# Two shared pools of PSUM slots and a new list of operations in a recurrence with a highway layer

## The chip, the core and the metric

The kernel runs on one core of a Trainium2 chip. The metric is device time in microseconds (us), the median over repeated runs. The engines are TensorE (PE: matmuls and transposes, results go to PSUM), VectorE (DVE), ScalarE (ACT), GpSimd (POOL), and SyncE (SP), which here only issues DMA transfers. Each engine works through its own queue in order and waits on semaphores for the others.

## What is computed

```python
sig = 1.0 / (1.0 + np.exp(-f_logit))          # x, f_logit: (4, 6336, 256)
f = lower_bound + (1.0 - lower_bound) * sig
i = 1.0 - f
for t in range(S):                            # for each of 4 sequences
    h = f[:, t] * h + i[:, t] * x[:, t]
    y[:, t] = h
H = np.maximum(y @ w_h, 0.0)                  # 25344 tokens of 256
T = 1.0 / (1.0 + np.exp(-(y @ w_t + b_t)))
out = T * H + (1.0 - T) * y
```

Inputs and output are float32. The recurrence runs along time, the highway layer works on each token by itself.

## The kernel before

The work is cut into 25 units: 24 of 1024 tokens (6 stretches of time for each of 4 sequences) and a last one of 768 that holds the rest of all four sequences. The channels (256) are two halves of 128 partitions. The first three units are cut into smaller pieces at the front (`CUTS`), the last into two pieces throughout.

With u = sigmoid(-f_logit), f = 1 - (1 - lower_bound) u and i x = (1 - lower_bound) u x. The factor (1 - lower_bound), `cc`, is taken out of the scan and put into the weights (`w_sb`) and a diagonal matrix (`diag`); `ncc` is its negative. Each step of a unit has a letter, and the string `PLAN` is a list of letters written out by hand: for each letter the next instance of that step is emitted, and `pin` keeps the emitted order on each engine. So `PLAN` gives the order of all five queues.

| letter | engine | step (line) |
|---|---|---|
| L, X, R | SP | load f_logit, load x (L106), store out (L297); Q: the weights (L120) |
| U | ACT | u = sigmoid(-f_logit), 128x2048 (L149) |
| P | POOL | bv = u x, four per unit (`product`, L155) |
| A, F | PE, ACT | transpose u into uT (L186), then f = 1 + ncc uT (L193); per half |
| B, S | PE, DVE | transpose bv into bT (L202), then the scan y = f y + bT (L217); per half |
| W | DVE | fold cc into the weights (L143), twice |
| Z, T | PE, ACT | zp = w_t y (L232), t = sigmoid(zp + b_t) (L238); per half |
| G, D | PE, DVE | gp = w_h y (L232), d = max(ncc y, gp) (L243); per half |
| E, H | DVE, POOL | e = d t, its columns divided between DVE (L258) and POOL (L155); both halves at once |
| O | PE | op = diag y + e, transposed back to tokens (L276, L277); two groups `q` of four blocks per unit |
| C, V | ACT, DVE | copy op to o (L291); V takes half of each copy in the last three pieces |

Before, each of the five kinds of product has one PSUM tile (`bufs=1`, tag = kind): uT and bT one bank each, zp, gp and op two banks each, eight in all. A product waits until the reader of the last one of its kind is done. `SHARE` is the number of columns of each half of e that POOL takes (448 of 1024; DVE takes the other 576, so a row of the profile has 2 x 576 = 1152). `gpsimd_mul` makes a POOL multiplication wait for DVE's e before it in the list. The pools in SBUF hold five f_logit tiles, five x tiles and eight o tiles. The DMA transfers share eight semaphores, so that each waits for the one eight before it.

Of the kernel before, what the change touches and what calls it, by code (L numbers as in the profile page):

```python
# [19 lines left out]
def kernel(  # L20
# [43 lines left out]

    HELPED = 3

    first = ctx.enter_context(tc.tile_pool(name="first", bufs=1))
# [14 lines left out]
    def pin(ins):  # L84
        return tc.keep_in_program_order(ins)

    def pairs(t):

        return t.rearrange("p (k j) d -> p k (j d)", j=2)

    def inner(t):

        return t.rearrange("p k d j -> p k j d")
# [1 line left out]
    def tokens(src, u, j0, j1, j):  # L95

        np_, _, b, per, a = units[u]
        if per == NB:
            return src[b, a + j0 * np_:a + j1 * np_, :].rearrange("(k p j) d -> p k (j d)", p=np_, j=j)
        return src[b + j0 // per:b + j1 // per, a:a + per * np_, :].rearrange("b (p j) d -> p b (j d)", j=per)  # L100

    def load(i, name, src):
        u, j0, j1 = fronts[i]
        np_ = units[u][0]
        t = fs[i][name] = new(name, [NB, D], FP32)
        pin(nc.sync.dma_start(pairs(t[:np_, :j1 - j0]), tokens(src, u, j0, j1, 2)))  # L106

    def shape(piece):

# [43 lines left out]
    def gpsimd_mul(out_, a, b):  # L153

        ins = pin(nc.gpsimd.tensor_mul(out_, a, b))  # L155
        while port:
            tc.add_manual_dep(ins.ins, port.pop().ins.name, mybir.DependencyInfo(
                mybir.DependencyClass.Sync, mybir.DependencyReason.DATA), reason="shared port")

    def product(i, k):  # L160
        np_, _ = shape(fronts[i])
        if k == 0:
            fs[i]["bv"] = new("bv", [NB // 2, D, 2], BF16)
        gpsimd_mul(inner(fs[i]["bv"][:np_, k:k + 1])[:, 0], fs[i]["u"][:np_, 2 * k:2 * k + 2],
                   fs[i]["xt"][:np_, 2 * k:2 * k + 2])

    def width(piece):
        np_, nb = shape(piece)
# [3 lines left out]

        return ((0,), (1,)) if width(piece) > 512 else ((0, 1),)

    def psum(piece, m, s, key, dtype):

        t = ps1.tile([P, NB * P], dtype, tag=key, name=key)
        for c, h in enumerate(halves(piece)[m]):
            s[key, h] = t[:, c * 512:c * 512 + width(piece)]
            yield s[key, h], h  # L180

    def decay_pe(i, m):
        np_, nb = shape(fronts[i])
        for uT, h in psum(fronts[i], m, fs[i], "uT", FP16):
            for j in range(nb):
                pin(nc.tensor.transpose(uT[:, j * np_:(j + 1) * np_], fs[i]["u"][:np_, j, h * P:(h + 1) * P],  # L186
                                        ident_h[:np_, :np_]))

    def decay_act(i, h):

        np_, N = shape(fronts[i])[0], width(fronts[i])
        f = fs[i]["f", h] = new("f", [NB * P], FP16)
        pin(nc.scalar.activation(f[:, :N].rearrange("p (k q j) -> p k q j", q=np_, j=2),  # L193
                                 fs[i]["uT", h].rearrange("p (k j q) -> p k q j", q=np_, j=2), AF.Identity,
                                 scale=ncc[:, h:h + 1], bias=1.0))

    def b_pe(i, m):
        np_, nb = shape(fronts[i])
        for bT, h in psum(fronts[i], m, fs[i], "bT", BF16):

            for k in range(nb // 2):
                pin(nc.tensor.transpose(bT[:, 2 * k * np_:2 * (k + 1) * np_].bitcast(FP32),  # L202
                                        fs[i]["bv"][:np_, k, h * P:(h + 1) * P].rearrange("p d j -> p (d j)").bitcast(FP32),
                                        ident_f[:np_, :np_]))

# [17 lines left out]
        u, j0, j1 = backs[j]  # L223
        return ys[u][:, :, j0 * units[u][0]:j1 * units[u][0]]

    def ffn_pe(j, m, key, k):
        N = width(backs[j])
        for p, h in psum(backs[j], m, bs[j], key, FP32):
            for ki in range(NH):
                for a in range(0, N, 512):  # L230
                    e = min(a + 512, N)
                    pin(nc.tensor.matmul(p[:, a:e], w_sb[:, k, ki, h * P:(h + 1) * P], y_of(j)[:, ki, a:e],  # L232
                                         start=ki == 0, stop=ki == NH - 1))
# [9 lines left out]
        pin(nc.vector.scalar_tensor_tensor(bs[j]["d"][:, m, :width(backs[j])], y_of(j)[:, m], ncc[:, m:m + 1],  # L243
                                           bs[j]["gp", m], op0=ALU.mult, op1=ALU.max))

    SHARE = 448

    def shared(j):

# [5 lines left out]
        return (bs[j][key][:, :, a:e] for key in "edt")  # L255

    def e_dve(j):
        port.append(pin(nc.vector.tensor_mul(*e_cols(j, 0, width(backs[j]) - shared(j)))))  # L258

    def e_pool(j):  # L260
        gpsimd_mul(*e_cols(j, width(backs[j]) - shared(j), width(backs[j])))

    QB = NB // 2

    def o_pe(j, q):

        op = bs[j]["op", q] = ps1.tile([P, QB, D], FP32, tag="op", name="op")
        (np_, nb), y = shape(backs[j]), y_of(j)
        j0, j1 = q * QB, min((q + 1) * QB, nb)
        g = min(j1 - j0, units[backs[j][0]][3])  # L270
        for k in range(j0, j1):
            b, i = divmod(k - j0, g)
            cols = slice((j0 + b * g) * np_ + i, (j0 + (b + 1) * g) * np_, g)
            for h in range(NH):
                o = op[:np_, k - j0, h * P:(h + 1) * P]
                pin(nc.tensor.matmul(o, y[:, h, cols], diag[:, h], start=True, stop=False))  # L276
                pin(nc.tensor.matmul(o, bs[j]["e"][:, h, cols], ident_b, start=False, stop=True))  # L277

    def copied(j, q):

        g = min(QB, shape(backs[j])[1] - q * QB)
        return g, g // 2 if j >= len(backs) - HELPED else g

    def o_copy(j, q, engine):
        np_ = shape(backs[j])[0]
        if ("o", q) not in bs[j]:
            bs[j]["o", q] = new("o", [QB, D], FP32)
        g, a = copied(j, q)
        part = slice(0, a) if engine is nc.scalar else slice(a, g)
        copy = nc.scalar.copy if engine is nc.scalar else nc.vector.tensor_copy  # L290
        pin(copy(bs[j]["o", q][:np_, part], bs[j]["op", q][:np_, part]))  # L291

    def store(j, q):
        u, j0, _ = backs[j]
        a, (g, _) = j0 + q * QB, copied(j, q)
        per = min(g, units[u][3])
        pin(nc.sync.dma_start(tokens(out_bsd, u, a, a + g, per),  # L297
                              bs[j]["o", q][:units[u][0], :g].rearrange("p (k j) d -> p k (j d)", j=per)))

    def each(pieces, count):  # L300
        return [(i, k) for i, piece in enumerate(pieces) for k in range(count(piece))]

    def groups(piece):
        return -(-shape(piece)[1] // QB)


    kinds = {
# [1 line left out]
        "X": (lambda i, _: load(i, "xt", x), each(fronts, lambda p: 1)),  # L309
        "Q": (lambda i, k: load_weights(k), [(0, 0), (0, 1)]),  # L310
        "U": (lambda i, _: gate(i), each(fronts, lambda p: 1)),
        "P": (product, each(fronts, lambda p: shape(p)[1] // 2)),
        "A": (decay_pe, each(fronts, lambda p: len(halves(p)))),
        "F": (decay_act, each(fronts, lambda p: NH)),
        "B": (b_pe, each(fronts, lambda p: len(halves(p)))),
        "S": (scan, each(fronts, lambda p: NH)),
        "W": (lambda i, h: weights(h), [(0, 0), (0, 1)]),
        "Z": (lambda j, m: ffn_pe(j, m, "zp", 1), each(backs, lambda p: len(halves(p)))),
        "T": (t_act, each(backs, lambda p: NH)),
        "G": (lambda j, m: ffn_pe(j, m, "gp", 0), each(backs, lambda p: len(halves(p)))),  # L320
        "D": (d_dve, each(backs, lambda p: NH)),
        "E": (lambda j, _: e_dve(j), each(backs, lambda p: 1)),
        "H": (lambda j, _: e_pool(j), [(j, 0) for j in range(len(backs)) if shared(j)]),
        "O": (o_pe, each(backs, groups)),
        "C": (lambda j, q: o_copy(j, q, nc.scalar), each(backs, groups)),
        "V": (lambda j, q: o_copy(j, q, nc.vector), [p for p in each(backs, groups) if p[0] >= len(backs) - HELPED]),
        "R": (store, each(backs, groups)),
    }

    PLAN = (  # L330
        "XLLXLXQQLXUUAPFFBAPSSUFFBASSWLLXLXPFFUPBAPFFUUPWSSLLXXLXPPGABZPPFFTDSSGABZUFFTDSSEAGBZFUFUTHPPPPPPDS"
        "SOGABZCFTDSSAOGHPPPPFABZDSUFCTGBZALLXLXXLLRUTUFDSBGEESDOZBAGCTUFSDPPPPHZOBASTCFGZOBAPPPPHTCFDSZGOABD"
        "ESTUCFGZOABTFCDZAGOHPPPPFTCSDEEAGBOZXXRRLRRRRLLXFUCTDSAGBOZDSPHPPPFCTAOBZGESDFCOBATUFPPPPHPPZGATFCSD"
        "BZGAOTFCUSDPPHBZGAOXRRXXLRXLRRRTFCSDEBGAZOFTCESDABZGOPPPPPPHFTUCSDABGZOSEDPPHFTCABZGOFTUCSDRRXLLXRRR"
        "XBZGAOSDTFCBAGOZPHPPPPSDEFUTCBAGZOSDFTCABZGOPPHPPSDEFTCXLLRRRRBGAOZESDUFCTBOAGZSPHPPPPPPUFTCBADSGZOB"
        "FTCDESAGOZBHPPPPUCFTDSOGAZBCTFDSOGZBAHPCTUFDEESGZOABXRRRXRLLXLLRRDSTFCPPPPPHZGAOBTFCDSZGOBAUTCDSPPPH"
        "ZGODEFTCUBZAGOFTCESDABZGOFTCUSDPPHPPHPPPABZGOSDRXRRLRRRLXTCFBZOAGSEDTCFBZAGOTUCFSDBZGOAPPPPPHTCSDEZB"
        "OGFCTAOESDPHPPUCBZGOSDFTCBAZGORRRXRRRRXPHPUFTCSDEBAGZOSDFFTCABZGOFTCPPHRRRSSDEZGOBTFCRDGOZHSDDESCROT"
        "TCEVRGZOTTCDDVROEVCROCVR"
    )  # L340
    assert all(PLAN.count(k) == len(places) for k, (_, places) in kinds.items())
    todo = {k: iter(places) for k, (_, places) in kinds.items()}
    for k in PLAN:
        kinds[k][0](*next(todo[k]))
# [1 line left out]
_INS = ['x', 'f_logit', 'lower_bound', 'moe_w_h', 'moe_w_t', 'moe_b_t']  # L346
_OUTS = [((25344, 256), 'float32')]
# [25 lines left out]
```

## Time and profile before

| | us |
|---|---|
| median of 8 runs | 220.27 (219.81 to 221.81) |
| the profiled execution, whole | 221.08 |
| its span in the profile | 219.3 |

| what | value |
|---|---|
| scan (L217, 128x1024), mean | 2340 ns x40 |
| d (L243, 128x1024), mean | 1259 ns x48 |
| e on DVE, 1152 columns | 760 ns x24 |
| e on POOL, 896 columns | 1944 ns x24 |
| product bv on POOL | 1176 ns x96 |
| u (L149, 128x2048) | 1954 ns x21 |
| f, t, copy on ACT (128x1024) | 1176, 1166, 1060 ns |
| bytes moved | 78.4 MB, 52.4 read and 26.0 written |

The span is from the first to the last instruction of the profiled execution. A line of the timeline gives the start in us, the duration in us, engine and line of the kernel, operation, output and inputs, shape and count; in brackets stands how long the engine was idle before it, and what ended the wait. Durations of neighbours on one engine overlap a little, so the distance from start to start is what an operation costs there.

### The profile page before, as it was taken

Reading aid. Unit: us, or ns where it says so; the run is one execution under the profiler, and the core shown is the slowest. Engines: PE = TensorE matmul, PEld = TensorE weight load, DVE = VectorE, ACT = ScalarE, POOL = GpSimd, SP = SyncE. Lnnn points to the kernel's source line nnn. Section 1 sums busy time; section 2 is a strip of 40 time slices with the busy share of each in tenths; the row PEclk is TensorE's granted clock in tenths of the full one; section 3 lists DMA queues with packets and bytes.
Section 4 is the critical chain, followed back from the end, with each engine's and each line's share of the span. In section 5 each row is a group of like instructions: output and inputs, shape, how many; then the busy total and the mean of one; then the engine's idle time right before and its main releaser. Section 6 shows DMA issues by size and latency. Waiting matters only on the chain.

```text
span 219.3 us, 4597 instructions
## 1 busy us (share of the span) xinstructions
PE 188.1 (86%) x1800; PEld 131.6 (60%) x1800; DVE 195.3 (89%) x154; ACT 195.2 (89%) x194; POOL 161.9 (74%) x136
## 2 busy tenths in 40 slices
PE   0478787799999999999999999999999978999840
PEld 0345463556766757666776676676667646766640
DVE  1298986999999999999999999999999996999931
ACT  2669999999999999999999999999999977997621
POOL 4566579699769698789986979599699869853200
PEclk9999999999999999999999999999999999999985
DMA  4999999999999999999999999999999993554553
GB/s 97 395 408 408 409 405 408 409 403 409 407 414 417 404 412 406 412 410 416 409 406 415 409 413 412 411 409 409 410 416 412 346 396 146 197 189 167 215 211 103
DMA packets 34741, 78.68 MB, mean 359 GB/s; under 512 B 2336, under 2 KB 2848, under 8 KB 34720
## 3 DMA queue, kind: packets, MB, share of 16 engines
q1 hardware_dynamic: 34176, 78.39, 92.3%
q8 instruction: 14, 0.23, 0.4%
q10 hardware_dynamic: 544, 0.00, 0.1%
q14 instruction: 7, 0.06, 0.1%
HBM read 52.43 MB, written 25.95 MB: 357 GB/s over the span
## 4 chain that ended last, share of the span: by engine, by line
PE 26%; DVE 20%; ACT 10%; DMA 5%; issue 4%; POOL 2%; DVEq 0%; ACTq 0%
DVE y L217 10%; PE gp L232 8%; DVE d L243 6%; PE zp L232 6%; DMA out_dram<-o 5%; PE op L276 3%; PE op L277 3%; ACT f L193 3%; PE bT L202 3%; ACT o L291 3%; PE uT L186 3%; ACT t L238 3%; DVE e L258 2%; POOL e L155 1%; DVE o L291 1%
## 5 line engine op out<-in xcount | busy, mean ns | idle before, releaser
L155 POOL TENSOR_TENSOR bv<-u,xt 128x512 bf16<-128x512 f16 (+1 forms) x100 | 114.4, 1176 | 31.4 <-DVE e L258 8.1
L217 DVE TENSOR_TENSOR_SCAN y<-f,y,bT 128x1024 bf16<-128x1024 f16 (+3 forms) x56 | 106.7, 1918 | 1.5 <-PE bT L202 1.4
L243 DVE SCALAR_TENSOR_TENSOR d<-y,ncc,gp 128x1024 bf16<-128x1024 bf16 (+1 forms) x52 | 62.7, 1208 | 4.3 <-PE gp L232 2.9
L193 ACT ACTIVATE f<-uT,ncc 128x1024 f16<-128x1024 f16 (+3 forms) x60 | 59.8, 1009 | 2.4 <-PE uT L186 2.4
L291 ACT COPY o<-op 128x1024 f32<-128x1024 f32 (+2 forms) x50 | 51.1, 1022 | 10.3 <-PE op L277 7.7
L238 ACT ACTIVATE t<-zp,bt 128x1024 bf16<-128x1024 f32 (+1 forms) x52 | 58.1, 1121 | 1.3 <-DVE o L291 0.8
L232 PEld LDWEIGHTS <-w_sb 128*128 128x128 f16 x400 | 38.0, 98 | 35.0 <-issue 3.9
L155 POOL TENSOR_TENSOR e<-d,t 128x896 bf16<-128x896 bf16 x24 | 46.7, 1944 | 10.1 <-DVE d L243 5.3
L232 PE MATMUL gp<-y,w_sb 128*128 128x512 bf16 (+1 forms) x200 | 51.9, 381 | 2.4 <-DVE d L243 1.5
L276 PE MATMUL op<-diag,y 128*128 128x128 f16 (+1 forms) x400 | 51.2, 221 | 3.3 <-ACT o L291 1.8
L277 PE MATMUL op<-ident_b,e 128*128 128x128 bf16 (+1 forms) x400 | 51.2, 221 | 3.0 <-POOL e L155 2.9
L149 ACT ACTIVATE u<-lt 128x2048 f16<-128x2048 f32 (+3 forms) x30 | 49.6, 1657 | 4.1 <-DMA lt<-in_f_logit_dram 3.7
L277 PEld LDWEIGHTS <-e 128*128 128x128 bf16 (+1 forms) x400 | 45.3, 115 | 11.1 <-issue 3.3
L232 PE MATMUL zp<-y,w_sb 128*128 128x512 bf16 (+1 forms) x200 | 50.9, 377 | 0.0
L276 PEld LDWEIGHTS <-y 128*128 128x128 bf16 (+1 forms) x400 | 45.5, 115 | 3.9
L186 PE MATMUL uT<-ident_h,u 128*128 128x128 f16 (+1 forms) x400 | 31.8, 224 | 9.6 <-ACT u L149 7.8
L202 PE MATMUL bT<-ident_f,bv 128*128 128x128 f32 (+1 forms) x200 | 32.5, 284 | 7.5 <-DVE y L217 5.1
L186 PEld LDWEIGHTS <-u 128*128 128x128 f16 (+1 forms) x400 | 26.9, 100 | 17.3 <-ACT u L149 9.1
L202 PEld LDWEIGHTS bT<-ident_f,bv 128*128 128x128 f32 (+1 forms) x200 | 22.0, 144 | 15.0 <-issue 5.5
L258 DVE TENSOR_TENSOR e<-d,t 128x1152 bf16<-128x1152 bf16 (+1 forms) x26 | 18.8, 744 | 0.5 <-ACT t L238 0.5
L217 DVE TENSOR_TENSOR_SCAN y<-f,bT 128x512 bf16<-128x512 f16 (+2 forms) x8 | 10.5, 1343 | 4.5 <-PE bT L202 4.5
L291 DVE COPY o<-op 128x512 f32<-128x512 f32 (+1 forms) x4 | 2.8, 689 | 4.8 <-DMA out_dram<-o 3.2
(19 smaller groups left out, 7.4 us busy)
## 6 DMA issues: line engine op xcount, KB each, us to landing
out_dram<-o SPq DMA_DIRECT2D x48, 512.0 KB, 11.4
lt<-in_f_logit_dram SPq DMA_DIRECT2D x21, 1024.0 KB, 14.0
xt<-in_x_dram SPq DMA_DIRECT2D x21, 1024.0 KB, 13.8
lt<-in_f_logit_dram SPq DMA_DIRECT2D x5, 512.0 KB, 8.0
xt<-in_x_dram SPq DMA_DIRECT2D x5, 512.0 KB, 9.1
lt<-in_f_logit_dram SPq DMA_DIRECT2D x2, 384.0 KB, 11.4
xt<-in_x_dram SPq DMA_DIRECT2D x2, 384.0 KB, 5.3
out_dram<-o SPq DMA_DIRECT2D x2, 384.0 KB, 3.0
```

The lines of the kernel that those rows point to most:

```text
L149: pin(nc.scalar.activation(u[:np_, :nb], fs[i]["lt"][:np_, :nb], AF.Sigmoid, scale=-1.0))
L155: ins = pin(nc.gpsimd.tensor_mul(out_, a, b))
L186: pin(nc.tensor.transpose(uT[:, j * np_:(j + 1) * np_], fs[i]["u"][:np_, j, h * P:(h + 1) * P], ident_h[:np_, :np_]))
L193: pin(nc.scalar.activation(f[:, :N].rearrange("p (k q j) -> p k q j", q=np_, j=2), fs[i]["uT", h].rearrange("p (k j q) -> p k q j", q=np_, ...
L202: pin(nc.tensor.transpose(bT[:, 2 * k * np_:2 * (k + 1) * np_].bitcast(FP32), fs[i]["bv"][:np_, k, h * P:(h + 1) * P].rearrange("p d j -> ...
L217: pin(nc.vector.tensor_tensor_scan(y, fs[i]["f", h][:, c:c + w], fs[i]["bT", h][:, c:c + w], 0.0 if prev is None else prev, op0=ALU.mult, ...
L232: pin(nc.tensor.matmul(p[:, a:e], w_sb[:, k, ki, h * P:(h + 1) * P], y_of(j)[:, ki, a:e], start=ki == 0, stop=ki == NH - 1))
L238: pin(nc.scalar.activation(bs[j]["t"][:, m, :width(backs[j])], bs[j]["zp", m], AF.Sigmoid, bias=bt[:, m:m + 1]))
L243: pin(nc.vector.scalar_tensor_tensor(bs[j]["d"][:, m, :width(backs[j])], y_of(j)[:, m], ncc[:, m:m + 1], bs[j]["gp", m], op0=ALU.mult, op1 ...
L276: pin(nc.tensor.matmul(o, y[:, h, cols], diag[:, h], start=True, stop=False))
L277: pin(nc.tensor.matmul(o, bs[j]["e"][:, h, cols], ident_b, start=False, stop=True))
L291: pin(copy(bs[j]["o", q][:np_, part], bs[j]["op", q][:np_, part]))
```

## The change

The five PSUM tiles become two pools of slots: two of one bank ("one0", "one1"), which uT and bT share, and three of two banks ("two0" to "two2"), which zp, gp and op share. The list has, after each letter of a product (A, B, Z, G, O), a digit that names its slot. A product waits until the reader of whatever was last in that slot is done. `SHARE` goes from 448 to 512. The list itself is new: order on all engines, and of the loads and stores.

```diff
-    def psum(piece, m, s, key, dtype):
-        t = ps1.tile([P, NB * P], dtype, tag=key, name=key)
+    def psum(slot, shape, key, dtype):
+        tag = ("one" if dtype in (FP16, BF16) else "two") + slot
+        return ps1.tile([P, *shape], dtype, tag=tag, name=key)
+
+    def filled(piece, m, slot, s, key, dtype):
+        t = psum(slot, [NB * P], key, dtype)
         for c, h in enumerate(halves(piece)[m]):
...
-    SHARE = 448
+    SHARE = 512
...
-    def o_pe(j, q):
-        op = bs[j]["op", q] = ps1.tile([P, QB, D], FP32, tag="op", name="op")
+    def o_pe(j, q, slot):
+        op = bs[j]["op", q] = psum(slot, [QB, D], "op", FP32)
...
-    for k in PLAN:
-        kinds[k][0](*next(todo[k]))
+    letters = iter(PLAN)
+    for k in letters:
+        kinds[k][0](*next(todo[k]), *([next(letters)] if k in "ABZGO" else []))
```

A stretch of each list from the middle, and both ends:

```diff
-        "XLLXLXQQLXUUAPFFBAPSSUFFBASSWLLXLXPFFUPBAPFFUUPWSSLLXXLXPPGABZPPFFTDSSGABZUFFTDSSEAGBZFUFUTHPPPPPPDS"
...
-        "FTCDESAGOZBHPPPPUCFTDSOGAZBCTFDSOGZBAHPCTUFDEESGZOABXRRRXRLLXLLRRDSTFCPPPPPHZGAOBTFCDSZGOBAUTCDSPPPH"
...
-        "OGFCTAOESDPHPPUCBZGOSDFTCBAZGORRRXRRRRXPHPUFTCSDEBAGZOSDFFTCABZGOFTCPPHRRRSSDEZGOBTFCRDGOZHSDDESCROT"
-        "TCEVRGZOTTCDDVROEVCROCVR"
+        "LLXLXXLXLQQUPXLXUA0B1PFFSSA0B1UFFLXPSSA0PLUFFUB1A0XPPLSSWWFFPPXXLB1A0Z0G1FUFTUPSSDPG2A1B0Z1PPFFTDSSU"
+        "B1A0Z0Z2G1ESSDHPPTFFG0A1B0PDSPSTFUHPPO1O2B1SCCA0G0Z1Z2B1FTTUDESG0A0O1O2FCCPPPDB1A0Z0G1G2ESRXLRLLXRXL"
...
+        "1ESRXRXRLRXXLRRLZ0G1A0Z2B1TFTUDSPHPPA0G0O1O2PFCCDB1A0FZ0G1Z2B0ESTTUHPPDSO0A1G1O2FCPPCDB0A1G1Z0Z2FTTU"
...
+        "G1Z0Z2B0FTTUDESPPA1G1O0O2FPPCCDB0LLXLXLRRRRRRRXRXSHA1G1Z0Z2B0FTTDESPPA1O1G0FDA1B0UFSHZ2Z0B1CTTEPPPSP"
...
+        "FFTDSZ2G1G0A0HTFSDDEZ2B1Z1O0FTTTSEHO2CSG1CRZ0RG2DTDTEDO1O0CVDVO1CERRCVO2RCVR"
```

In the middle the old list has, on ACT, the pattern f, t, copy again and again with a sigmoid now and then; on PE bT, zp, gp, uT, op per half. The new list has, per unit, on ACT f, copy, copy, f, t, t, sigmoid, and on PE the six large products as Z, G, Z and then G, O, O over the three slots. On SP the loads begin with two f_logit pieces instead of x, the weights come after the second unit's first pieces, and stores of the units come in groups with loads between.

The rest of the diff adds settings that leave things as they are here: `run` gives 2 for every piece, so the loads, `decay_act` and `b_pe` are laid out as before; `LASTQ` = 4 equals `QB`; `EARLY` is empty, so no product moves to DVE; `o_copy` takes the same ranges as before.

## The prediction

> **What bounds it now.** I read the engine shares first, then the windows of busy time, then the timelines of VectorE and ScalarE in the middle, and last the timeline of the end.
>
> ```profile
> PE 188.1 (86%) x1800; PEld 131.6 (60%) x1800; DVE 195.3 (89%) x154; ACT 195.2 (89%) x194; POOL 161.9 (74%) x136
> ```
> ```profile
> 0.00:10.00 10.00, 1.72 (x10) 1.13 (x10) 2.26 (x8) 4.92 (x8) 4.79 (x14) 1.00 0.73 232
> ...
> 40.00:178.00 138.00, 132.54 (x1303) 93.48 (x1301) 137.42 (x91) 137.48 (x127) 115.70 (x92) 1.00 1.04 408
> 178.00:219.30 41.30, 29.86 (x311) 21.93 (x309) 30.14 (x34) 25.49 (x32) 18.97 (x13) 0.91 0.51 190
> ```
>
> The columns are length, then busy time of PE, weight loads, DVE, ACT, POOL, then clock, DMA share and GB/s. From 40 to 178 us both DVE and ACT work without a gap, and the DMA moves 408 GB/s all the time. An 89% average hides that: there is nothing to win in the middle except by less work on *both* engines. Free time lies in the first 40 us and the last 41 (DVE idle 11.2 there).
>
> ```profile
> 101.89 2.04 ACT L149 ACTIVATE u<-lt 128x2048 f16<-128x2048 f32 x1
> 103.70 1.15 ACT L291 COPY o<-op 128x1024 f32<-128x1024 f32 x1
> 104.59 1.27 ACT L238 ACTIVATE t<-zp,bt 128x1024 bf16<-128x1024 f32 x1
> 105.60 1.27 ACT L193 ACTIVATE f<-uT,ncc 128x1024 f16<-128x1024 f16 x1
> 106.59 1.17 ACT L291 COPY o<-op 128x1024 f32<-128x1024 f32 x1
> ```
> ```profile
> 98.14 0.73 DVE L258 TENSOR_TENSOR e<-d,t 128x1152 bf16<-128x1152 bf16 x1
> 98.79 1.27 DVE L243 SCALAR_TENSOR_TENSOR d<-y,ncc,gp 128x1024 bf16<-128x1024 bf16 x1
> 99.98 2.34 DVE L217 TENSOR_TENSOR_SCAN y<-f,y,bT 128x1024 bf16<-128x1024 f16 x1
> 102.24 1.25 DVE L243 SCALAR_TENSOR_TENSOR d<-y,ncc,gp 128x1024 bf16<-128x1024 bf16 x1
> ```
>
> Durations overlap, so I count from start to start. ACT: sigmoid u 1.81 (103.70 - 101.89), copy 0.89, t 1.01, f 0.99. One unit of 1024 tokens needs one u and two of each other: 7.59 us. DVE: scan 2.26, d 1.18, e 0.65: two scans, two d and one e are 7.53. TensorE by the chain's rows (four matmuls of 512 columns 0.86, eight transposes 0.45, four of bT 0.44) and 16 small matmuls of op 0.055 apart (0.89): 4 x 0.86 + 2 x (0.45 + 0.44 + 0.89) = 7.0. So ACT leads by little, and PE has 0.6 us of room per unit.
>
> **SHARE 448 to 512.** 64 columns of each half, 128 elements, go from DVE's e to POOL's. DVE rows: 1152 take 760 ns and 768 take 552, so 0.54 ns each, 0.07 us for each of 24 units, 1.7 in all. It is hidden: ACT's 7.59 does not shrink, so in the middle I count 0. POOL's e grows from 1944 ns by 128/896 to 2.22 us; with four products at 1.14 (4.55 for four) its unit is 6.8 of 7.59, still covered by 0.8. If that cover goes, every 0.1 us over it costs 17 x 0.1 in the middle.
>
> A rule bears on this. The Trainium skill, "SBUF — State Buffer", section "Who interferes with whom", says that a DVE instruction with two SBUF inputs and a POOL instruction that reads SBUF hold a shared read port in turn, the later one waiting. The nearest row is POOL's e at 178.40, beside a pair of DVE e's (1.42): 3.14 where the others take 1.89, so 1.25 lost. By the rule, a longer POOL e meets more DVE e's: if each of 24 did, 30 us more on POOL, 1.25 per unit, beyond its 0.8. But the list puts each POOL e behind its own DVE e and the next is a unit away; the mean over 24 is 1944, so few collide. I take the row's mean: no cost.
>
> **Slots.** Before, uT, bT, zp, gp and op each own one PSUM slot. After, uT and bT share two, zp, gp and op share three, six big tiles per unit in the order Z G Z, G O O. I followed one unit of the new list by hand with the durations above. From a sigmoid's end at 0, ACT ends f at 1.0, two copies at 1.9 and 2.8, f at 3.8, two t at 4.8 and 5.8, the next sigmoid at 7.6. PE has uT for the first f ready 2.3 before 0 and the first op 0.6 before, the second at 0.3. When the first f has freed its slot (1.0) come uT (to 1.5) and Z (2.4); G has its slot from the first copy (1.9) and ends at 3.2, the second Z from the second copy (2.8) and ends at 4.1; ACT wants it at 4.8. That 0.7 us is the least margin. DVE runs d, scan, d, e, scan; each bT is refilled beneath a d (1.18), as before. So the middle stays at ACT's rate: 0. New waits sit on PE's transposes, Z, G and O; behind a late one all later PE work queues, and both ACT and DVE wait for that. Their price has no row; bounds: 0 if they fit in the 0.6 us of room, 0.1 to 0.2 for each of ten groups per unit (PE rows after a wait: 0.34 to 0.52 idle) if they do not. I take 0, since the hand-made unit shows the margins.
>
> A second rule speaks against it: "TensorE: Matmul & The Clock Gate", section "A second HAM failure mode: psum-queue depth-cycling", says that cycling matmul groups through PSUM banks with small idle gaps can make the clock drop and recover. This trace already cycles through eight banks and has granted clock 1.00 from 40 to 178. By the rule at half clock PE's unit would be 14 us and the middle twice as long; by the row nothing. I take the row, as PE stays over 90% busy.
>
> **Order of loads and head.** SP's list now begins with two f_logit pieces, and x of unit 3 comes before f_logit of unit 4; the first store waits behind x and f_logit of unit 5. DMA time is (MB ahead)/0.408 + 4.2 us (0.53 MB had moved by 5.5), and a landing lags that: x of unit 3 had 9.97 MB up to its end, so 28.6, and POOL started on it at 30.87. In the new order only 8.9 MB lie before it: 2.6 us sooner. The weights' two DVE steps (0.74 each) move behind the third piece's scans and are no longer in a gap: 1.4 on the path. Followed by hand, DVE ends unit 3's second scan at 39.3, where before starts it at 39.29; an e (0.65) is done earlier too, a d (1.18) is still owed: 2.26 + 0.65 - 1.18 = 1.7 ahead, of which I count 1.5. ACT gains nothing: f_logit of unit 5 has 13.1 MB up to its end, 36.3 + 2 = 38.3, and ACT is there at 36.5. From there 7.59 per unit bring it to unit 20's first t at 172.1, or at 174 if it loses the 1.9 us that before lost on the way (from 69.10 it took 102.6 us for 100.7 us of work). Before starts that t at 171.66, with one copy (0.89) less behind it. So ACT is between 0.5 ahead and 1.4 behind, and the later engine counts: **+1.0** (ends -1.5 and +1.4).
>
> Later loads: f_logit of unit 17 has 50.3 MB before its end, 127.5 + 2; ACT reaches it at about 129. Stores issued in runs of up to seven cost SP waiting, but eight transfers stay in flight. So DMA is level with ACT and 0 more.
>
> **Tail.** Here the one op slot is what ends last:
>
> ```profile
> 209.69 0.22 PE L276 MATMUL op<-diag,y 128*96 128x128 f16 x1 [1.40 <-DVE o L291]
> ...
> 212.14 0.26 PE L276 MATMUL op<-diag,y 128*96 128x128 f16 x1 [1.39 <-ACT o L291]
> ```
> ```profile
> 209.56 0.55 DVE L258 TENSOR_TENSOR e<-d,t 128x768 bf16<-128x768 bf16 x1
> 210.78 0.69 DVE L291 COPY o<-op 96x512 f32<-96x512 f32 x1 [0.68 <-PE op L277]
> 214.65 0.69 DVE L291 COPY o<-op 96x512 f32<-96x512 f32 x1 [3.18 <-DMA out_dram<-o]
> ```
>
> Each op group waits until both copies of the last one are done. With slots 1, 0, 1, 2 for the last four, the last e no longer waits for a copy: d ends 208.2, e 208.8, op 0.9, ACT copy 0.6, DVE copy 0.7 give 211.0 in place of 215.34: **-4.3**. The collision at 178.40 (DVE idle 1.41 at 183.46) goes with its place in the list: -1.4. Waits of 0.52 and 0.45 at 185.26 and 200.63 may go: -0.5. New short waits for G and O of the last units: +1.2. The store and the end after the last copy (219.3 - 215.34 = 4.0) stay.
>
> Sum: 1.0 - 4.3 - 1.4 - 0.5 + 1.2 = -4.0, so span 215.3. The profiled run took 221.08 for its span of 219.3, 0.8 above the median 220.27; against that median: **216.3**.
>
> **Rivals.** (1) *Slot release stalls PE* (slower): in the middle, PE waiting over 0.6 us per unit sets the rate. Past that each 0.1 costs 17 x 0.1 = 1.7; 0.24 more eats the 4.0. At ten waits of 0.11 us (1.1) it is +0.5 x 17 = 8.5 on the forecast: 225. For it: PE at 132.5 of 138 us busy. Against: 0.7 us margins. (2) *Loads eat the tail's gain*: ACT or SP late by 3 to 4 us in total, at units 5, 14 and 17, where margins are about 1: 220. For it: 408 GB/s unbroken. (3) *The slots do little*: uT and bT still alternate as if each owned one, and only half of the tail's gain comes: 218.5.
>
> **Numbers.** Forecast 0.64, rival 1 0.19, rival 2 0.11, rival 3 0.06. A measurement tells some 0.3% (0.7 us) from no change. Forecast and rival 3 are faster; of rival 2, 0.04 each way, 0.03 same; of rival 1 nearly all slower. Faster 0.73, same 0.05, slower 0.22. Range: best, DVE's 1.5 ahead counts and the tail gives 6.2, with no new waits: 212.6; up, rival 2 and the start of rival 1: 221.5. The forecast's own range is 212.6 to 218.5.
>
> **What would show it.** Right: ACT and DVE again full from 40 to about 175, PE clock 1.00, DVE e near 0.69, and the last two op groups with no wait for a copy. Wrong: PE rows waiting for copies or d in the middle, DVE waiting for gp or bT there, ACT waiting for lt beyond 40 us, or POOL's e above 2.3.

## The result and the profile after

| | us | |
|---|---|---|
| before, in the same session | 220.56 | 219.76 to 223.14 |
| changed kernel, median of 18 runs | 218.81 | 217.08 to 219.79 |
| its profiled execution, whole | 217.08 | span 215.1 |
| ratio to before | 0.9913 | 95% interval 0.9893 to 0.9933 |

The change gains 0.9%; the forecast was 216.3 against 220.27, a ratio of 0.982. So the sign is right, and just under half of the gain came. Note the third row: the profiled execution is the shortest of the 18 runs. Its span of 215.1 agrees with the forecast's 215.3 almost to the digit, and that agreement is luck: this run is not typical, and two terms of the forecast missed in opposite directions (see the section on the prediction).

First the engine shares of the changed kernel:

```profile
PE 187.2 (87%) x1800; PEld 131.3 (61%) x1800; DVE 195.9 (91%) x154; ACT 194.5 (90%) x194; POOL 168.2 (78%) x136
```

The work of VectorE and ScalarE is as before; only the span is shorter. The windows of the changed kernel (same columns as those of before) say where:

```profile
10.00:40.00 30.00, 24.72 (x197) 16.85 (x198) 27.01 (x24) 25.13 (x28) 25.00 (x20) 1.00 1.05 406
40.00:178.00 138.00, 131.11 (x1278) 91.51 (x1276) 135.85 (x91) 136.84 (x127) 118.92 (x90) 1.00 1.04 400
178.00:215.10 37.10, 29.66 (x321) 21.86 (x319) 30.87 (x34) 27.17 (x33) 19.42 (x14) 0.95 0.61 239
```

The end is 4.2 us shorter (37.10 against 41.30) for as much work. In the middle the clock is 1.00 and both engines are nearly full, as before; but ACT now misses 1.2 us there (0.5 before), and the DMA moves 400 GB/s instead of 408. Those two small numbers are the trace of what went wrong.

The timeline of ScalarE in the middle shows one unit of the new list (f, two copies, f, two t, u):

```profile
100.23 2.16 ACT L154 ACTIVATE u<-lt 128x2048 f16<-128x2048 f32 x1
102.03 1.36 ACT L205 ACTIVATE f<-uT,ncc 128x1024 f16<-128x1024 f16 x1
103.03 2.18 ACT L303 COPY o<-op 128x1024 f32<-128x1024 f32 x2
104.83 1.40 ACT L205 ACTIVATE f<-uT,ncc 128x1024 f16<-128x1024 f16 x1
105.87 2.36 ACT L251 ACTIVATE t<-zp,bt 128x1024 bf16<-128x1024 f32 x2
107.88 2.17 ACT L154 ACTIVATE u<-lt 128x2048 f16<-128x2048 f32 x1
```

From one u to the next it is 7.65 us, and no row is followed by a bracket: ScalarE waits for no slot. At the end, the timeline of VectorE:

```profile
207.75 0.55 DVE L166 TENSOR_TENSOR e<-d,t 128x768 bf16<-128x768 bf16 x1
208.97 0.69 DVE L303 COPY o<-op 96x512 f32<-96x512 f32 x1 [0.67 <-ACT o L303]
210.05 0.69 DVE L303 COPY o<-op 96x512 f32<-96x512 f32 x1 [0.39 <-ACT o L303]
```

The last e starts at 207.75 and the last copy ends at 210.74, 3.0 us after it; before, the last e started at 209.56 and the last copy ended at 215.34, 5.8 us after it. The 3.18 us wait in front of the last copy is gone.

Now what the forecast did not have. The queue of SyncE in the changed kernel, near unit 0's first store:

```profile
18.59 4.89 SPq L106 DMA_DIRECT2D xt<-in_x_dram  x2
23.57 2.40 SPq L106 DMA_DIRECT2D lt<-in_f_logit_dram  x1
34.34 0.36 SPq L309 DMA_DIRECT2D out_dram<-o  x1
34.79 0.39 SPq L106 DMA_DIRECT2D xt<-in_x_dram  x1
35.23 0.86 SPq L106 DMA_DIRECT2D lt<-in_f_logit_dram  x1
```

SP finishes issuing f_logit of unit 5 at 25.97. The next in its queue is the store of unit 0's first group, whose copy is not made before 34.3. For 8.4 us SP issues no transfer, although x and f_logit of unit 6 stand behind the store, and two more f_logit tiles behind the next one. The windows of the changed kernel show the DMA running dry shortly after:

```profile
38.00:40.00 2.00, 2.00 (x34) 1.80 (x32) 2.00 (x1) 2.00 (x2) 1.99 (x2) 1.00 1.04 404
40.00:42.00 2.00, 1.75 (x26) 1.51 (x24) 1.90 (x3) 2.00 (x3) 1.50 (x2) 1.00 1.06 323
42.00:44.00 2.00, 2.00 (x11) 0.90 (x10) 2.00 (x2) 2.00 (x3) 1.74 (x1) 1.00 0.91 272
44.00:46.00 2.00, 2.00 (x29) 1.69 (x28) 2.00 (x3) 1.28 (x3) 2.00 (x3) 1.00 1.03 409
```

The last number is GB/s. In 4 us (408 - 323) x 2 + (408 - 272) x 2 = 442 KB are not moved, 1.1 us of DMA time. ScalarE's timeline shows who pays:

```profile
45.89 1.92 ACT L154 ACTIVATE u<-lt 128x2048 f16<-128x2048 f32 x1 [0.72 <-DMA lt<-in_f_logit_dram]
...
173.72 1.01 ACT L303 COPY o<-op 128x1024 f32<-128x1024 f32 x1 [0.44 <-DMA out_dram<-o]
174.62 2.13 ACT L251 ACTIVATE t<-zp,bt 128x1024 bf16<-128x1024 f32 x2
```

f_logit of unit 6 is 0.72 us late; a wait of ScalarE for f_logit beyond 40 us is one of the signs of being wrong that the prediction names. Much later a copy of unit 18 waits for the o tile that a store of unit 14 still has to empty; that store was queued behind six loads.

### The profile page after: what moved, and what is told of

It reads as the page before. It is cut to its first block, busy times and chain, and to the rows that moved or that the text cites. A ratio compares the mean times of both kernels' runs of the same rounds, so it can differ in the third digit from the quotient of the medians.

```text
span 215.1 us, 4591 instructions
## 1 busy us (share of the span) xinstructions
PE 187.2 (87%) x1800; PEld 131.3 (61%) x1800; DVE 195.9 (91%) x154; ACT 194.5 (90%) x194; POOL 168.2 (78%) x136
## 4 chain that ended last, share of the span: by engine, by line
ACT 45%; DMA 24%; PE 10%; issue 9%; DVE 7%; POOL 2%; SPq 0%; ACTq 0%; DVEq 0%; POOLq 0%
ACT t L251 13%; ACT f L205 12%; ACT o L303 11%; DMA xt<-in_x_dram 10%; ACT u L154 9%; DMA out_dram<-o 7%; DMA lt<-in_f_logit_dram 5%; DVE y L230 4%; PE zp L245 3%; PE gp L245 2%; PE uT L198 2%; DMA lb<-in_lower_bound_dram 2%; DVE d L256 1%; PE bT L215 1%; POOL bv L160 1%
## 5 line engine op out<-in xcount | busy, mean ns | idle before, releaser
L160 POOL TENSOR_TENSOR bv<-u,xt 128x512 bf16<-128x512 f16 (+1 forms) x100 | 115.8, 1180 | 20.9 <-DVE e L166 8.0
L205 ACT ACTIVATE f<-uT,ncc 128x1024 f16<-128x1024 f16 (+3 forms) x60 | 64.1, 1083 | 4.0 <-PE uT L198 4.0
L160 POOL TENSOR_TENSOR e<-d,t 128x1024 bf16<-128x1024 bf16 x24 | 51.1, 2129 | 14.6 <-DVE e L166 11.8
L251 ACT ACTIVATE t<-zp,bt 128x1024 bf16<-128x1024 f32 (+1 forms) x52 | 56.9, 1192 | 1.9 <-PE zp L245 0.9
L154 ACT ACTIVATE u<-lt 128x2048 f16<-128x2048 f32 (+3 forms) x30 | 52.1, 1736 | 5.5 <-DMA lt<-in_f_logit_dram 5.1
L303 ACT COPY o<-op 128x1024 f32<-128x1024 f32 (+2 forms) x50 | 49.9, 1116 | 2.8 <-DVE o L303 1.9
L245 PE MATMUL gp<-y,w_sb 128*128 128x512 bf16 (+1 forms) x200 | 50.3, 377 | 0.8 <-ACT t L251 0.8
L296 PE MATMUL op<-diag,y 128*128 128x128 f16 (+1 forms) x400 | 49.2, 219 | 1.9 <-ACT o L303 0.8
L297 PE MATMUL op<-ident_b,e 128*128 128x128 bf16 (+1 forms) x400 | 49.1, 219 | 0.9 <-DVE e L166 0.5
L166 DVE TENSOR_TENSOR e<-d,t 128x1024 bf16<-128x1024 bf16 (+1 forms) x26 | 18.4, 712 | 1.9 <-ACT t L251 0.6
```

The costliest lines, as they stand in the source:

```text
L154: pin(nc.scalar.activation(u[:np_, :nb], fs[i]["lt"][:np_, :nb], AF.Sigmoid, scale=-1.0))
L251: pin(nc.scalar.activation(bs[j]["t"][:, m, :width(backs[j])], bs[j]["zp", m], AF.Sigmoid, bias=bt[:, m:m + 1]))
L303: pin(copy(bs[j]["o", q][:np_, a:e], bs[j]["op", q][:np_, a:e]))
```

## The experiments

My theory (A) was that the sum over the engines holds, and that a store placed in front of loads on SP's queue takes the rest of the gain. The rivals (B) differ from run to run and stand in the expectations. "The changed kernel" is the one above; ratios are to the kernel before, run beside it.

| run | median us | ratio, 95% interval |
|---|---|---|
| changed kernel again | 218.41 | 0.9903 (0.9865 to 0.9941) |
| unit 0's stores later | 216.50 | 0.9812 (0.9776 to 0.9849) |
| last stores dealt out among loads | 217.10 | 0.9823 (0.9784 to 0.9861) |
| both moves | 216.13 | 0.9786 (0.9747 to 0.9824) |
| kernel before, first store early | 222.50 | 1.0082 (1.0053 to 1.0112) |
| kernel before, last two op groups in free slots | 218.81 | 0.9927 (0.9892 to 0.9963) |
| changed, last four op groups in one slot | 222.49 | 1.0049 (1.0011 to 1.0087) |
| changed, zp, gp, op in own slots, units 4 to 17 | 267.68 | 1.2083 (1.2001 to 1.2164) |
| changed, uT and bT in own slots, units 4 to 19 | 221.44 | 1.0011 (0.9964 to 1.0058) |
| the same, units 4 to 17 | 218.97 | 0.9925 (0.9893 to 0.9956) |
| changed, SHARE 448 | 218.68 | 0.9902 (0.9864 to 0.9940) |

### The changed kernel again

No edit.

> The changed kernel itself once more, for its spread and a second profile; nothing is left out. If its profiled execution (span 215.1) was merely the fastest of 18, this one has a span of 216 to 218, and the extra time sits in waits for f_logit (units 5 to 8, and around unit 17) that follow the late first store. If the extra time comes from PSUM slots, TensorE shows waits for copies or d of more than 0.6 us per unit between 50 and 160 us instead, and ScalarE's unit is over 7.7 us there. Ratio to before about 0.991 either way.

218.41 us, and a profile at 218.75, which is a typical run where the first profile was not. Its span is 216.7. The wait of unit 18's copy in its ScalarE timeline:

```profile
172.57 1.28 ACT L205 ACTIVATE f<-uT,ncc 128x1024 f16<-128x1024 f16 x1
175.27 1.01 ACT L303 COPY o<-op 128x1024 f32<-128x1024 f32 x1 [1.42 <-DMA out_dram<-o]
176.18 2.12 ACT L251 ACTIVATE t<-zp,bt 128x1024 bf16<-128x1024 f32 x2
```

The first data landed 0.77 us later in this execution (ScalarE's first 1024-wide sigmoid at 8.74, not 7.97), and at unit 20's t it is 1.56 behind the first profile: the store wait grew from 0.44 to 1.42. Its DMA lost more near 40 us too (38 to 44 us: 320, 293, 258 GB/s, 1.7 us of DMA time against 408). I had expected waits for f_logit as well; there is none beyond 40 us, and all of the loss shows at the store wait.

### Unit 0's stores behind the loads

On SP's part of the list, no other engine's order touched:

```diff
-RXLRLLXRXL
+XLLRRXLRXL
```

> The new list with one stretch of SP's queue changed: the two stores of unit 0 go behind x of unit 6 and f_logit of units 6 and 7. Nothing else moves on any engine. Theory A (the first store holds SP from 26 to 34 us, the DMA runs dry near 40 us, and f_logit of unit 6 is late, by more in some executions than in others): no wait for f_logit of unit 6, no dip of the GB/s near 40 us, span 213 to 214.5, median 216 to 217, smaller spread, ratio to before 0.980 to 0.986. Theory B (the shortfall comes from elsewhere, or what is saved is lost again at a later wait): same as the changed kernel within 0.5 us, ratio 0.989 to 0.993.

The windows of this run:

```profile
38.00:40.00 2.00, 2.00 (x31) 1.70 (x29) 2.00 (x2) 2.00 (x2) 1.79 (x2) 1.00 1.05 409
40.00:42.00 2.00, 1.76 (x28) 1.59 (x27) 1.90 (x3) 2.00 (x3) 1.70 (x2) 1.00 1.05 409
42.00:44.00 2.00, 2.00 (x14) 0.94 (x12) 2.00 (x2) 2.00 (x3) 1.55 (x1) 1.00 1.06 413
```

The dip is gone, so is ScalarE's wait for f_logit of unit 6 (u at 45.20 without a bracket), and the time is 216.5: two stores moved behind three loads bring 2 us. This is the forecast's time, though not by the forecast's terms. The copy of unit 18 still waits 0.50. It starts at 173.03 here, without the hole; at 173.72 in the first profile of the changed kernel, whose hole is 1.1 us; and at 175.27 in the second, with 1.7 us and a later start. So in these three profiles the store that it waits for lands later with the hole.

### The last stores dealt out among the last loads

```diff
-LLXLXLRRRRRRRXRX
+LRLRXRLXLRRRRXRX
```

> The changed kernel; on SP alone the last run of seven stores is dealt out among the last loads (order L22, store 14.0, L23, store 14.1, X22, store 15.0, L24a, ... in place of five loads and then seven stores). The two stores of unit 0 stay where the new list has them, in front of x and f_logit of unit 6. Theory A (SP held by a store early makes the DMA lose 1 to 2 us near 40 us, and the bill is paid where ACT's copy of unit 18 waits for the o tile of store 14.0, 0.44 to 1.42 us in the two profiles of this list): that wait goes, about 1 us less, ratio 0.984 to 0.988. Theory B (the lateness comes from the first loads or from the order on the engines, the store wait only shows it): the wait goes but the time stays, 0.990 to 0.993.

> Both moves on SP: the stores of unit 0 behind x of unit 6 and f_logit of units 6 and 7, and the last seven stores dealt out among the last loads. Theory A: the remaining 0.50 us wait of the copy of unit 18 goes as well, no other wait comes: 0.976 to 0.980. Theory B (DMA has no slack at the end, so a store moved forward makes a load late): 0.981 or above, with a new wait of ACT for f_logit of unit 22 or 23.

Alone it gives 217.10, somewhat more than I expected: the early dip is still there (323 and 308 GB/s from 35 to 45 us), and ScalarE waits 0.51 us for f_logit of unit 6, but at the copy of unit 18 there is no wait any more. With both moves, the ScalarE timeline:

```profile
172.61 1.19 ACT L303 COPY o<-op 128x1024 f32<-128x1024 f32 x1
173.50 2.32 ACT L251 ACTIVATE t<-zp,bt 128x1024 bf16<-128x1024 f32 x2
```

No bracket. 216.13 us is the fastest version found, 2.1% below before; no wait for f_logit of unit 22 or 23 came in its place. The two moves are not additive (by the medians, 2.1 us for unit 0's stores and 1.5 for the last stores, against 218.6, the middle of the changed kernel's two medians, and 2.5 together; by the ratios 2.1, 1.9 and 2.7), as they should not be: both concern the same lost DMA time, one avoids it, the other avoids one place where it is paid. Between the single moves and both, the intervals overlap, so the runs do not split the loss between the two places.

### The same fault put into the kernel before

In the kernel before, the first store stands behind f_logit of unit 10. Here it goes to the place it has in the new list:

```diff
-X3 L5 X4 L6 L7 X5 L8 X6 X7 L9 L10 R0.0
+X3 L5 R0.0 X4 L6 L7 X5 L8 X6 X7 L9 L10
```

(These are the names of SP's operations, with their units.)

> The kernel before with one store moved on SP: the first store of unit 0 directly behind f_logit of unit 5 and in front of x of unit 4, as the new list has its first store behind f_logit of unit 5 in front of a load. Its copy ends at 30.3 in the trace of before, and SP would be there at 21.1, so SP is held for about 9 us. Theory A (a store in front of loads lets the DMA run dry): below 400 GB/s somewhere between 30 and 36 us and 1 to 2 us slower, 1.004 to 1.010. Theory B (the loads are far enough ahead): no dip, 0.998 to 1.002.

1.8 us slower by the ratio. SP waits from 21.6 to 30.8; three windows of this run, and the middle one in the kernel before:

```profile
30.00:32.00 2.00, 1.45 (x11) 0.80 (x11) 2.00 (x3) 2.00 (x3) 1.09 (x1) 1.00 0.92 362
32.00:34.00 2.00, 2.00 (x28) 1.55 (x26) 0.96 (x1) 2.00 (x3) 2.00 (x3) 1.00 0.90 256
34.00:36.00 2.00, 1.41 (x14) 1.05 (x14) 1.34 (x2) 2.00 (x2) 2.00 (x3) 1.00 0.92 345
...
32.00:34.00 2.00, 2.00 (x28) 1.53 (x26) 0.68 (x2) 2.00 (x3) 2.00 (x3) 1.00 1.05 410
```

The kernel before moves 408 to 410 GB/s there (last row). ScalarE then waits 2.88 us for f_logit at 41.38. So the store's place costs time in either list.

### What the slots are worth at the end

The old list and SHARE 448, written as slots (uT 0, bT 1, zp 0, gp 1, op 2), with only the last two op groups moved:

```diff
-O2EVCRO2CVR
+O0EVCRO1CVR
```

> The list and SHARE of before, with uT, bT, zp, gp and op each in a slot of its own as before, but for the last two op groups, which go into zp's and gp's slot. Theory A (half of the tail's gain is the one op slot): the last op group waits for no copy, the last VectorE copy ends about 2.6 us earlier (212.7 against 215.3), ratio 0.987 to 0.990. Theory B (the end is set by the copies and the last store, whatever the slots): ratio 0.997 to 1.000.

218.81, as fast as the changed kernel, with two letters. In the profile the last copy ends at 212.74 instead of 215.34. The reverse, on the changed kernel, puts its last four op groups into slot two1, all other orders kept:

```diff
-O1O0CVDVO1CERRCVO2RCVR
+O1CVO1DVCO1ERRCVO1RCVR
```

> The changed kernel with the last four op groups all in slot two1 (1, 1, 1, 1 in place of 1, 0, 1, 2), so that each waits for both copies of the one before; order on all engines as in the changed kernel. Theory A (the shared slots at the end are worth what the list before lost there): 2.0 to 3.5 us slower than the changed kernel, ratio 1.000 to 1.007. Theory B (the new order of the last steps alone gives the gain, the slots hardly any): within 0.7 us of the changed kernel, 0.989 to 0.994.

Slower than the changed kernel by 3.7 to 4.1 us by the medians, which is beyond the 3.5 that I gave, and by 3.1 by the ratios, which is inside. TensorE's timeline in this run has the waits of before back:

```profile
208.34 0.22 PE L296 MATMUL op<-diag,y 128*128 128x128 f16 x1 [1.40 <-DVE o L303]
...
210.80 0.27 PE L296 MATMUL op<-diag,y 128*96 128x128 f16 x1 [1.40 <-ACT o L303]
...
214.06 0.26 PE L296 MATMUL op<-diag,y 128*96 128x128 f16 x1 [1.39 <-DVE o L303]
```

The waits bring a second cost, which neither the forecast nor the expectation had. The windows of this run, and one of the kernel before:

```profile
206.00:208.00 2.00, 0.95 (x16) 0.84 (x16) 1.43 (x3) 1.52 (x3) 0.00 (x0) 1.00 0.79 315
214.00:216.00 2.00, 1.86 (x16) 1.65 (x15) 0.00 (x1) 0.04 (x1) 0.00 (x0) 0.50 0.54 154
...
212.00:214.00 2.00, 1.86 (x16) 1.65 (x15) 0.00 (x0) 0.09 (x1) 0.00 (x0) 0.50 0.50 139
```

The granted clock, third number from the right, is down to 0.50 in the last op group of the kernel before and in the last two here. The matmuls of such a group start 0.107 us apart instead of 0.055, so its 16 are begun within 1.55 us instead of 0.84: 0.7 us more for each group. With only the last two groups of the old list moved, the clock is 1.00 to the end of the matmuls (211.4). In this execution the way from unit 20's first t to the last copy's end is 41.0 us (176.23 to 217.26), where the changed kernel takes 36.1. Of these 4.9 us some 1.4 are clock.

### What the slots are worth in the middle

All orders on the engines, the loads and the tail are those of the changed kernel; in units 4 to 17 zp always takes two0, gp two1, op two2. For the products of one unit in TensorE's order (letters of the other engines left out):

```diff
-Z0G1Z2
+Z0G1Z0
...
-G0O1O2
+G1O2O2
```

> The changed kernel; in units 4 to 17 every zp goes to slot two0, every gp to two1, every op to two2, as if each kind owned its tile again. The order on all five engines is that of the changed kernel, and so are SHARE, the loads and the tail. Theory A (the new order of the list needs the shared slots; the middle stayed at ACT's 7.6 us per unit because of them): the second zp waits for t of the first and the second op for its copy, so ACT stands about 0.9 us before the second t and 0.9 before the second copy of each of 14 units: 15 to 30 us slower than the changed kernel, ratio 1.06 to 1.13. Theory B (the slots are worth something only at the end): within 1 us of the changed kernel, 0.987 to 0.996.

49 us slower than the changed kernel: the direction of Theory A, and half as much again as its upper end. ScalarE's timeline in this run:

```profile
103.02 1.11 ACT L205 ACTIVATE f<-uT,ncc 128x1024 f16<-128x1024 f16 x1
104.01 1.01 ACT L303 COPY o<-op 128x1024 f32<-128x1024 f32 x1
106.17 1.01 ACT L303 COPY o<-op 128x1024 f32<-128x1024 f32 x1 [1.14 <-PE op L297]
107.08 1.12 ACT L205 ACTIVATE f<-uT,ncc 128x1024 f16<-128x1024 f16 x1
108.84 1.11 ACT L251 ACTIVATE t<-zp,bt 128x1024 bf16<-128x1024 f32 x1 [0.65 <-PE zp L245]
111.07 1.11 ACT L251 ACTIVATE t<-zp,bt 128x1024 bf16<-128x1024 f32 x1 [1.11 <-PE zp L245]
112.08 1.90 ACT L154 ACTIVATE u<-lt 128x2048 f16<-128x2048 f32 x1
113.89 1.10 ACT L205 ACTIVATE f<-uT,ncc 128x1024 f16<-128x1024 f16 x1
```

From f to f it is 10.87, 3.3 above the changed kernel: three waits, not the two I named. The first zp is late as well: on TensorE the second op waits for the first copy until 105.08 (2.27 us), and uT, bT, gp and the first zp follow it without a gap to 108.7. 14 units of 3.3 are 46 of the 49 us. This profiled execution is the longest of the five (270.67 us), and some of its units are up to 12.4 us long, with a fallen clock in them (last section). The list with the pairs "copy, copy" and "t, t" only keeps its pace because the second product has another slot than the first.

The one-bank pool is another matter. uT always in one0, bT in one1, units 4 to 19 (here unit 6):

```diff
-A1B0A1B1
+A0B1A0B1
```

> The changed kernel; in units 4 to 19 every uT goes to slot one0 and every bT to one1, nothing else changed and all orders kept. Theory A (sharing uT and bT only swaps which of two readers each waits for, ScalarE's f or VectorE's scan): within 1 us of the changed kernel, 0.986 to 0.996. Theory B (the second pool matters as much as the first): 3 us or more slower, above 1.003, with VectorE waiting for bT or ScalarE for uT in each unit.

221.44, some 3 us slower, between the two theories and nearer to B. But 13 unit lengths of the middle take 99.8 us, where the changed kernel takes 99.4, and the trace shows the loss at one place, on TensorE:

```profile
164.99 0.74 PE L198 MATMUL uT<-ident_h,u 128*128 128x128 f16 x7 [2.78 <-DVE y L230]
```

This is where my edit ends: unit 20's first uT gets a slot that unit 19's last bT still holds. So the run was made again with an end where the slots fit:

> As the run with uT and bT in slots of their own from unit 4 to 19, but only to unit 17, where the changed list hands the slots over without a mixed pair; in the earlier run the first uT of unit 20 landed in a slot that the last bT of unit 19 still held, and ScalarE and VectorE stood some 4 to 5 us there at 161 to 172 us, while the 13 unit lengths before took 99.8 us against 99.4 in the changed kernel. Theory A (that seam is all of the loss, sharing uT and bT is worth nothing in the middle): within 1 us of the changed kernel, 0.987 to 0.996, and no wait of 0.7 us or more between 160 and 172. Theory B (the sharing is worth the loss): above 0.999.

218.97, the changed kernel's time within the intervals. Its 13 unit lengths take 99.8 us again, so sharing uT and bT is worth at most 0.4 us in the middle; the three two-bank slots are what the list needs.

### SHARE alone

```diff
-    SHARE = 512
+    SHARE = 448
```

> The new list and slots with SHARE back at 448. Theory A (ScalarE sets the middle, so VectorE's 0.07 us per unit is hidden): same as the changed kernel within 0.4 us, ratio 0.990 to 0.993. Theory B (VectorE sets it): 24 x 0.07 = 1.7 us slower, ratio 0.998 to 1.000. Theory C (the longer GpSimd e delays bT): faster than the changed kernel by 0.5 us or more, ratio under 0.989.

218.68: no difference.

## Why the prediction was half right

**What bounds it: right.** ScalarE's unit is 7.6 us in the middle of the changed kernel (99.4 us for 13), hardly less than before (7.7, by the 102.6 us that the prediction counts), the granted clock is 1.00, and all gain is outside.

**SHARE at 0: right.** 218.68 against 218.41 and 218.81. DVE's e fell to 0.69 us as computed (the median of its rows); POOL's e is 2.13, a little below my 2.22, and no one of the 24 exceeds 2.14, so the port collision priced at 1.25 does not occur on POOL. Once it looks as if it fell on DVE: the e at 186.52, begun while a product of POOL was running, took 1.27 us. That is one e of 24.

**Slots at 0 in the middle: right, and rival 1 wrong.** The hand-made unit held: no ScalarE wait for a slot from 50 to 170 us. The run with own slots shows what the margin of 0.7 us protected: with it gone the time is 267.7.

**Tail, -4.3 - 1.4 - 0.5 + 1.2 = -5.0: right in kind, 1.7 us too small.** The term for the head ends at unit 20's first t on ScalarE, so the tail is counted from there. To the last copy's end it is 36.1 us in the changed kernel (174.62 to 210.74), 36.1 in the second profile (176.18 to 212.27) and 36.3 with both store moves (173.50 to 209.81). Before it was 42.8, with the copy counted that was still owed (172.55 to 215.34): -6.7. Which of the terms was too small was not tested. The slots' own part, put at 4.3, was 3.1 to 4.1 when taken out of the new list and 2.0 when put into the old (220.84 to 218.81, the run of before beside it; 1.6 by the ratio), where the last d and copies still stand in another order. The clock of 0.50 in before's last op group, 0.7 us, is in the 4.3 without being named.

**Order of loads and head, +1.0 with later loads "0 more": this step failed.** It can be measured at the first t of unit 20, in the timeline of ScalarE before:

```profile
171.66 1.11 ACT L238 ACTIVATE t<-zp,bt 128x1024 bf16<-128x1024 f32 x1
```

Before starts it at 171.66 with one copy (0.89) less done. The changed kernel starts it at 174.62 in the first profile and 176.18 in the typical one, so it is 2.1 and 3.6 us behind, not 1.0. With both store moves it starts at 173.50: 0.95 behind, which is the +1.0. That it fits to 0.05 is chance, as the first data alone land up to 0.8 us apart from run to run. So the sum of the loads' bytes was sound as long as SP keeps issuing; GpSimd started on x of unit 3 2.4 and 1.1 us sooner than before in the two profiles (28.50 and 29.77, not 30.87), where I had 2.6. Less than VectorE's lead of 1.7 was there: it ended unit 3's second scan at 40.1 and 41.4 in the two profiles, not at 39.3. What failed is the sentence "Stores issued in runs of up to seven cost SP waiting, but eight transfers stay in flight". I had noted that the first store waits behind x and f_logit of unit 5, and read it only from the side of the store. I did not ask when its copy would be ready (34.3) and when SP would be there (26), nor what is behind it on the same queue. The transfers already issued last until about 40 us; from there the DMA has a hole of 1.1 to 1.7 us, and as it is full from 45 to 160 us, the hole is never made up and is still there at unit 18. (From 160 to 170 us the DMA drops once more, to 318 GB/s, while SP works through seven stores.) The same sentence passed over the seven stores behind six loads: dealt out among the loads, they too bring 1.5 to 1.9 us.

**Rival 2 had the mechanism in part.** "Loads eat the tail's gain, ACT or SP late" is what happened, but at unit 6 and at a copy of unit 18 instead of units 5, 14 and 17, and for about 2 us instead of 3 to 4. Rival 3's time of 218.5 is what was measured, yet that is luck: of its reasons the one on uT and bT held (218.97 with slots of their own), but the slots at the end are worth 3 to 4 us and the two-bank slots in the middle 49.

**From one execution to the median.** I took 0.8 off since before's profiled run lay above its median. That does not carry over: the changed kernel's first profiled run lies 1.7 below its median, the second (218.75) at it. In the 64 executions of the kernel before that ran beside the experiments, 19 had a mean granted clock of 0.99 or more and took 219.8 to 220.4 us, 31 had 0.98 to 0.986 and took 220.4 to 222.1. The profiled one has 0.983, with the half clock in the last op group. The changed kernel's profiles have 1.00 until their matmuls end, so there was nothing to take off.

**How the sum adds up.** In the typical profile the changed kernel is 3.6 us behind at unit 20's t, gains 6.7 from there to the last copy, and takes 0.4 us more after it (4.4 for 4.0): -2.7, and the spans differ by 2.6 (219.3 and 216.7). In the first profile it is 2.1 - 6.7 + 0.4 = -4.2, near the forecast's -4.0 because the head was 1.1 worse and the tail 1.7 better. Without the two misplaced groups of stores, 0.95 - 6.5 + 0.5 gives about -5.0 (spans 219.3 and 214.3), and the median of 216.13 meets the forecast's 216.3 only since the better tail and the 0.8 that should not have been taken off nearly cancel.

The first profile and the second also differ from each other: a start later by 0.77 us became 1.6 us later at unit 20's t, with a store wait of 1.42 instead of 0.44. The spread of the runs fits this reading: 217.1 to 219.8 for the changed kernel, 215.9 to 216.6 with both moves. That the later start itself causes the larger wait was seen in two profiles only.

## What to carry to other kernels

When loads and stores share an issuing queue, a store's place must be costed from behind: when is its data ready, when does the queue get to it, and which loads stand behind it for how long, against how many microseconds of transfers are already issued. Pooled PSUM slots and an order of work are one design: the same order cost 49 us without the pool in the middle, while at the end two letters of the slot list gave the old order as much as the whole change gained. Agreement of a total says little while its terms can miss in opposite directions: each term needs a point in the trace where it can be read. And a span that matches the forecast in one profile is no confirmation until the profiled run is placed among the others.

## What the runs showed of the hardware

The granted clock of TensorE fell in these runs after idle stretches of a few us, though not after every one. In the kernel before with its first store early, TensorE works about 1 us of the 4 from 40 to 44, in waits of at most 1.50 us each; the windows of that run:

```profile
40.00:42.00 2.00, 0.50 (x7) 0.28 (x4) 2.00 (x2) 0.62 (x1) 2.00 (x3) 1.00 1.05 410
42.00:44.00 2.00, 0.53 (x4) 0.19 (x3) 0.88 (x1) 2.00 (x2) 1.90 (x2) 1.00 1.05 408
44.00:46.00 2.00, 2.00 (x14) 1.37 (x14) 1.67 (x2) 2.00 (x3) 0.00 (x0) 0.70 1.05 408
46.00:48.00 2.00, 1.91 (x12) 1.31 (x12) 2.00 (x2) 2.00 (x3) 1.44 (x2) 0.50 1.07 410
```

The clock (third number from the right) is 0.70 and 0.50 in the 4 us after the idle stretch. The run with own slots for zp, gp and op shows the same in its middle (0.61 and 0.53 from 72 to 76 us, after 4 us of which TensorE worked 1.9, with one wait of 2.11 us), and there it recurs: 0.67 and 0.50 from 82 to 86. But in the kernel before TensorE works 1.8 of the 4 us from 178 to 182, with one wait of 2.10, and the clock stays at 1.00. So these traces give no length of wait and no share of idle time from which the clock falls. The prediction weighed a rule of the Trainium skill, "TensorE: Matmul & The Clock Gate", section "A second HAM failure mode: psum-queue depth-cycling": groups of matmuls that cycle through PSUM banks with small idle gaps make the clock drop and come back. In the changed kernel nothing of it is seen (1.00 throughout the middle, TensorE 95% busy, five pooled slots). With the same products in another assignment of slots the clock does fall, but so it does where the slots are those of before and TensorE waits for data (the windows above). The falls shown here come after waits of 1.3 us and more; whether cycling adds to them no run here shows.
